# Weight sums of a Strassen-like product: DMA accumulation and ScalarE negatives in place of GpSimd and VectorE subtractions

## The chip, the cores and the metric

The kernel runs on one core of a Trainium2 chip. Such a core has a matrix engine (TensorE, PE in the profile, with its weight loads as PEld), three elementwise engines (VectorE or DVE, ScalarE or ACT, GpSimd or POOL), a queue that only issues transfers (SyncE, SP) and 16 DMA engines. Each engine takes its instructions in order. The metric is the device time of one execution in microseconds (us); lower is better.

## The reference, cut to what matters

The first half is a state-space scan over `x` of 4 batches x 8 heads x 768 tokens x 32, in chunks of 32 tokens; its output is laid out as 3,072 tokens x 256 features. The second half is a feed-forward block, and only its last product matters for the change:

```python
h = x @ w_in                                   # 3072 x 256  times  256 x 2048
g = np.where(h > 0.0, h, np.exp(np.minimum(h, 0.0)) - 1.0)
return (g @ w_out).astype(np.float32)          # 3072 x 2048 times 2048 x 256
```

`w_out` is float32, 2048 x 256.

## The kernel before, in words

The tokens are worked through in twelve blocks of 256, numbered n = 0 to 11; from n = 2 on two blocks go as a pair. For each pair the kernel computes the scan (decays, scores, state sums and products, on all engines), then the first product `l1` / `l1_words` (L663, L781), the activation in several steps on ScalarE and VectorE, and the second product with `w_out`. The weights come in by DMA as pieces, are rounded and recombined on ScalarE, VectorE and GpSimd, and stay in SBUF.

The second product has two forms. Blocks 0 and 1 use `l2` (L828), an ordinary accumulation over 16 slices of `w_out`, each slice 128 x 256. All later pairs use `second` (L874), which splits `w_out` into quarters a11, a12, a21 and a22 (each of 8 rows of 128 x 128, 128 features by 128 columns; L724 and L725: an even or odd slice, and its left or right half of columns) and multiplies seven combinations in place of eight quarters, in the manner of Strassen's method as Winograd wrote it. It needs four sums of weights, computed once:

- s1 = a21 + a22, written over a21
- s2 = s1 - a11
- s3 = a11 - a21 (with the old a21)
- s4 = a12 - s2

s2, s3 and s4 lie in three new tiles of 128 x 8 x 128 (`weight_sums`, L720), s1 in the place of a21. `l2` still reads the old a21, so row i of s1 can only be written after block 1's `l2(1, i)`.

The order of the work is written out by hand. The code around the change is:

- the loop over j = 0 to 7 (L1179): blocks 2 and 3 through `l1`, block 0 through `l2(0, j)`, the last weight pieces, and the scan of the pair 4, 5 ahead (`scan_ahead`, L1147: with `decay`, whose exponentials are L525 on ScalarE and whose masks are L530 on GpSimd). After j = 7 come `words_of_w(5)` and `low_of_w(5)` (L735, L745), which split a piece of `w_in` into words; the latter is two subtractions on GpSimd (L851).
- the loop over j = 8 to 15, i = j - 8 (L1231): the pair 2, 3 through `l1_words`, block 1 through `l2(1, i)`, at i = 0 the scaling of B for blocks 4 and 5 (`scaled`, L406, GpSimd's L412, into the tile b_tok), at i = 2 their scores, state sums (`sums`, matmuls of L575 from b_tok) and states (L592 on VectorE, L597 on GpSimd), and at i = 4 and 5 their outputs (`across` L608 and `inside` L628, with the copies L655 to yT on ScalarE). At i = 7 `words_of_y(4)` and `both_of_y(4)` (L766, L776 on VectorE) turn yT into words for the next pair.
- the loop for n = 4 and on (L1312): the pair n through `l1_words` while `second(n - 2)` runs in steps (`l2s`). Its seven products per half are numbered r = 0 to 6 and use a11, a12, s1, s2, s3, a22 and s4 in that order; the first half takes rows 0 to 3 of each, the second rows 4 to 7. The additions to its results are L888 on VectorE.

In the kernel before, `differences` (L1175) puts s3's rows on GpSimd at i = 0, 2, 3 and 5; `sum_weights` (L709) puts the other three sums of row i on GpSimd at i = 0 to 5; and the rows 6 and 7 are left to VectorE in the loop for n = 4, two steps at each of k = 2, 3 and 4 (`left`, L1289, and L1325). All of them are TENSOR_TENSOR instructions of 128 x 128. Each `l1_words` is followed by L799, L808 and L809 on ScalarE and L802 and L816 on VectorE, for the activation.

Of the kernel before, what the change touches and what calls it, by code (L numbers as in the profile page):

```python
# [14 lines left out]
ALU = mybir.AluOpType  # L15
ACT = mybir.ActivationFunctionType
# [16 lines left out]
def kernel(  # L33
# [27 lines left out]
    nc = tc.nc  # L61
# [30 lines left out]
    for k in range(4):  # L92
        (nc.scalar if k % 2 else nc.sync).dma_start(
            out=la0[BH * k:BH * (k + 1)],
            in_=a.rearrange("b h (c s) -> (b h) c s", s=P)[:, 0:2, :])
# [187 lines left out]
    for v in range(2):  # L283
        nc.gpsimd.affine_select(
            out=low16[Q * v:Q * v + Q], in_=low16[Q * v:Q * v + Q], pattern=[[1, Q]],
# [5 lines left out]
        out=hmask, in_=hmask, pattern=[[-N, NH]], compare_op=ALU.is_ge, fill=0.0,  # L291
        base=0, channel_multiplier=1)
    nc.gpsimd.affine_select(
        out=hmask, in_=hmask, pattern=[[N, NH]], compare_op=ALU.is_ge, fill=0.0,
# [8 lines left out]
        out=minus, in0=ident, scalar1=-1.0, scalar2=None, op0=ALU.mult)  # L303
# [213 lines left out]
    def decay(n, q):  # L517

        decay_of(n, 2 * q)
        decay_of(n, 2 * q + 1)  # L520
# [165 lines left out]
    def elu():  # L686
        if not begun:
            begin_elu()
        n, i, ps = lag.pop(0)
        e = begun.pop()  # L690
        nc.scalar.activation(e, e, ACT.Exp, scale=-1.0)
        g_of[n, i] = ffn.tile([P, 2, BLK], F32, tag=f"g{n % 2}", name="g", bufs=12)
        nc.vector.scalar_tensor_tensor(
            out=g_of[n, i], in0=e, scalar=1.0, in1=ps,
            op0=ALU.subtract, op1=ALU.max)
# [10 lines left out]

    def sum_weights(eng, a, s, i):  # L709
        for step in weight_steps(eng, a, s, i):  # L710
            step()

    def weight_steps(eng, a, s, i):
        a11, a12, a21, a22 = (part[:, i] for part in a)
        s2, _, s4 = (part[:, i] for part in s)
        for out, in0, in1, op in (
                (a21, a21, a22, ALU.add), (s2, a21, a11, ALU.subtract), (s4, a12, s2, ALU.subtract)):
            yield lambda: eng.tensor_tensor(out=out, in0=in0, in1=in1, op=op)

    def weight_sums():  # L720
        return [conv.tile([P, MC // 2, P], F32, tag="w64", name="w_sum", bufs=W_AHEAD)
                for _ in range(3)]

    w_parts = w_out.rearrange("p (i k) (r c) -> p k r i c", k=2, c=P)  # L724
    a_out = [w_parts[:, k, r] for r in range(2) for k in range(2)]  # L725
    s_out = []
# [8 lines left out]
    def words_of_w(i):  # L735

        w = pieces[i][0]
        k_words[i] = conv.tile(
            [P, 2, KC, CW], F32R, tag="w64", name="w_words", bufs=W_AHEAD)
        nc.scalar.activation(k_words[i][:, 0], w, ACT.Copy, scale=NEAR)  # L740
        nc.vector.scalar_tensor_tensor(
            out=k_words[i][:, 1], in0=k_words[i][:, 0].bitcast(F32), scalar=1.0 / WORD - 1.0,
            in1=w, op0=ALU.mult, op1=ALU.add)

    def low_of_w(i):  # L745

        w0 = conv.tile([P, KC, CW], F32R, tag="w_in", name="w0", bufs=DF // CW + 1)
        for k in range(KC):
            sub(w0[:, k], pieces[i][0][:, k], k_words[i][:, 0, k].bitcast(F32))
        k_words[i] = k_words[i], w0  # L750
# [99 lines left out]
    def sub(out, in0, in1):  # L850
        nc.gpsimd.tensor_tensor(out=out, in0=in0, in1=in1, op=ALU.subtract)  # L851
# [120 lines left out]
    def w_take(i, low):  # L972

        w_abs(i)
        w_low(i, low)
        w_sign(i)

    def w_give(i):

        w_high(i)  # L980
        w_sum(i)
# [190 lines left out]
            at = k // 2 * 2 + late  # L1172
            turn_part(*[(m, 0), (m, 1), (m, 2), (m + 1, 0), (m + 1, 1), (m + 1, 2), (m, 3), (m + 1, 3)][at])

    def differences(i, count):  # L1175
        for r in range(i, i + count):
            sub(s_out[1][:, r], a_out[0][:, r], a_out[2][:, r])

    for j in range(2 * DIRECT):  # L1179
        n, i = 2 + j // DIRECT, j % DIRECT  # L1180
        if j < 7:
            l2(0, j)
        piece = todo < len(pieces) and j != 1
        if j == 0:
            elu()
        if piece:
            w_take(todo, nc.vector)
        l1(n, i)
        if j == 7:
            l2(0, j)  # L1190
        if j == 0:
            scaled(3, nc.gpsimd)
            turn(3)
            elu()
            turn_exp(3)
        if piece:
            w_give(todo)
            todo += 1
        while lag:
            elu()  # L1200
        if j == 4:
            w_take(todo, nc.scalar)
            w_give(todo)
            todo += 1
        if j == 0:
            decay(3, 2)
            decay(3, 3)
        if j == 1:
            scores(3)
            sums(3)  # L1210
            for q in range(4):
                weigh(3, q)
        if j == 2:
            states(3)
        if j == 3:
            inside(across(3), 3)
        if j == 4:
            words_of_y(2)
        if j == 4:
            words_of_w(4)  # L1220
        if j == 5:
            low_of_w(4)
        if j == 5:
            both_of_y(2)
        scan_ahead(j)
        if j == 3:
            s_out[:] = weight_sums()
        if j == 7:
            words_of_w(5)
            low_of_w(5)  # L1230
    for j in range(8, 16):  # L1231
        i = j - 8
        l1_words(2, j, between=4 if i == 7 else None)
        for p in ((), (6,), (), (7,), (0,), (1,), (2,), ())[i]:
            words_of_w(p)
        for p in ((), (), (6,), (7,), (0,), (), (), ())[i]:
            low_of_w(p)
        if i == 7:
            l2(1, 6)
            l2(1, 7)  # L1240
        begin_end()
        if i == 0:
            turn_part(5, 2)
            scaled(4, nc.gpsimd)
            scaled(5, nc.gpsimd)
        if i < 2:
            load_bc(i + 6)
            l2(1, i)
        if i == 2:
            l2(1, 2, half=0)  # L1250
            scores(4, 5)
            sums(4, 5)
            for q in range(4):
                weigh_two(4, q)
            l2(1, 2, half=1)
            states(4)
            states(5)
            turn_part(4, 3)
            turn_part(5, 3)
            for to in (6, 7):  # L1260
                load_b(to)
                spread_cum(to)
        if i == 3:
            l2(1, 3)
        if i == 4:
            y = across(4, 5)
            inside(y, 4, 5, ts=(0,))
            l2(1, 4)
        if i == 5:
            l2(1, 5, half=0)  # L1270
            inside(y, 4, 5, ts=(1,))
            l2(1, 5, half=1)
        if i in (0, 1, 3, 4):
            sum_t1(2, (0, 1, 3, 4).index(i), nc.vector)
        if i in (4, 6):
            turn_part(6, i // 2 - 2)
        if i in (0, 2, 3, 5):
            differences((0, 0, 2, 4, 0, 6)[i], 2)
        if i < 6:
            sum_weights(nc.gpsimd, a_out, s_out, i)  # L1280
    end_words()
    for p in (1, 2):
        low_of_w(p)
# [2 lines left out]
    low_of_w(3)  # L1286
    sum_t2(2, 0)
    sub(g_of[2, 14][:, 1], g_of[2, 14][:, 1], g_of[2, 14][:, 0])
    left = (step for i in (6, 7) for step in weight_steps(nc.vector, a_out, s_out, i))  # L1289

    def stage_scan(n, k):

# [19 lines left out]
    for n in range(4, NP, 2):  # L1312
        m = n + 2 if n + 2 < NP else None
        steps = second(n - 2)

        def l2s(count):
            for _ in range(count):
                next(steps)

        for k in range(16):  # L1320
            l1_words(n, k, between=m if k == 15 else None)
            turn_step(n, k // 2 * 2 + 1, k % 2)
            if n == 4 and k == 0:
                decay(6, 1)
            if n == 4 and 1 < k < 5:  # L1325
                for _ in range(2):
                    next(left)()
            if m:
                stage_scan(n, k)
            begin_end()  # L1330
            if k == 0 and n > 4:
                store(n - 4, 0)
                store(n - 4, 1)
            if not m:
                l2s(4 if k % 2 else 3)
                continue
            l2s((3 + (n == 4), 3 - (n == 4), 3, 3, 3, 3, 3, 3, 4, 5, 2, 2, 3, 1, 1, 0)[k])
            if k == 9:
                scores(m, m + 1)
                sums(m, m + 1)  # L1340
                for q in range(4):
                    weigh_two(m, q)
                l2s(2)
                states(m)
            if k == 10:
                states(m + 1)
            if k == 13:
                y = across(m, m + 1)
                inside(y, m, m + 1, ts=(0,))
                l2s(4)  # L1350
                inside(y, m, m + 1, ts=(1,))
        if m:
            l2s(4)
            both_of_y(m)
        end_words()
        for _ in steps:
            pass
    n = NP - 2
# [34 lines left out]
```

## Time and profile before

| | |
|---|---|
| median of 3 runs | 350.58 us (350.37 to 350.59) |
| profiled execution | 350.72 us, of it 348.8 us span |
| granted TensorE clock | 0.999 |
| GpSimd: 8 subtractions for s3 (L851, w_sum<-w_out) | 4.3 us, 552 ns each |
| GpSimd: 18 sums at L718 | 3.6 + 3.4 + 3.1 us, 605, 567 and 524 ns each |
| VectorE: 6 sums at L718 | 125.7 to 133.1 us |
| first product with s2 (ps_o<-w_sum,t) | 126.4 us |
| first product with s3 (ps_o<-w_sum,g) | 130.6 us |
| busy from 87 to 100 us: PE, DVE, ACT, POOL | 12.56, 12.07, 6.29, 12.60 us of 13 |
| busy from 100 to 115 us | 14.67, 12.88, 11.73, 14.37 us of 15 |
| busy from 115 to 125 us | 9.83, 7.00, 8.25, 9.78 us of 10 |
| busy from 125 to 135 us | 9.30, 9.93, 8.46, 9.77 us of 10 |

The span runs from the first to the last instruction of the profiled execution. Busy times say how full an engine is in a stretch; for TensorE the ends of instructions are modelled, so full means that no idle time was seen. Times in timelines count from the start of the span. A line such as L851 can be that of a helper, so groups are told apart by their tiles: `w_sum<-w_out` are the weight sums, `w<-w_in,w_words` the low words of `w_in`, `g<-g`, `t<-g`, `g<-t,g` and `g<-g,t` the sums of activations for `second`.

### The profile page before, as it was taken

The numbers are of one execution on the slowest core, as the hardware profiler recorded it, in microseconds if no ns is written. First come the engines' busy times: TensorE is split into PE (matmuls) and PEld (weight loads), VectorE is DVE, ScalarE is ACT, GpSimd is POOL, SyncE is SP. The second block draws the span as 40 slices with busy tenths as digits, with TensorE's granted clock in tenths as the row PEclk, the third lists the DMA queues.
The fourth block names the chain that finished last, engine by engine and source line by source line (L and its number), as shares of the span: only waits on it lengthen the run. The fifth ranks groups of instructions, "written<-read, shape, count | busy, mean of one in ns | idle before, by whom it ended". The sixth has DMA issues, their size and how long they took to land.

```text
span 348.8 us, 9876 instructions
## 1 busy us (share of the span) xinstructions
PE 340.7 (98%) x3878; PEld 298.3 (86%) x3878; DVE 258.5 (74%) x514; ACT 235.2 (67%) x538; POOL 219.4 (63%) x338
## 2 busy tenths in 40 slices
PE   8999999999999999999999999999999999999996
PEld 5669888888878788888999988998988999999996
DVE  3998989879987799875878775888675756665232
ACT  4789989599748789647699447699557566665000
POOL 5554554558999998964196864196854174455860
PEclk9999999999999999999999999999999999999999
DMA  8988988551360601080431070320000100001002
GB/s 148 238 217 181 309 187 226 123 93 43 65 137 2 131 22 31 7 156 12 103 64 32 8 158 6 95 44 2 2 0 5 62 0 3 0 0 43 22 0 62
DMA packets 72727, 26.49 MB, mean 76 GB/s; under 512 B 57768, under 2 KB 67560, under 8 KB 72680
## 3 DMA queue, kind: packets, MB, share of 16 engines
q1 hardware_dynamic: 70360, 25.60, 31.6%
q8 instruction: 30, 0.49, 0.6%
q10 hardware_dynamic: 2320, 0.26, 0.5%
q14 instruction: 17, 0.14, 0.1%
HBM read 22.51 MB, written 3.34 MB: 74 GB/s over the span
## 4 chain that ended last, share of the span: by engine, by line
PE 80%; DVE 7%; ACT 6%; SPq 2%; DMA 2%; issue 2%; POOL 0%; DVEq 0%; ACTq 0%; POOLq 0%
PE ps_o L910 32%; PE ps_h L791 16%; PE ps_h L671 11%; PE ps_w L791 8%; PE ps_o L835 6%; PE ps_y L638 2%; DVE ps_h L802 2%; DMA w<-in_moe_w_in_dram 2%; ACT e L809 1%; ACT e L808 1%; PE ps_g L545 1%; PE ps_y L620 1%; PE ps_st L575 1%; ACT e L799 1%; ACT L L525 1%
## 5 line engine op out<-in xcount | busy, mean ns | idle before, releaser
L910 PEld LDWEIGHTS ps_o<-w_out,g 128*128 128x128 f32 x640 | 78.6, 191 | 3.6 <-ACT p_sum L922 0.2
L910 PE MATMUL ps_o<-w_out,g 128*128 128x128 f32 x640 | 80.3, 275 | 0.0
L808 ACT ACTIVATE e<-ps_h 128x512 f32<-128x512 f32 x72 | 43.0, 597 | 53.5 <-DVE ps_h L802 53.5
L816 DVE SCALAR_TENSOR_TENSOR g<-e,ps_h 128x512 f32<-128x512 f32 x72 | 49.3, 685 | 30.6 <-ACT e L809 30.1
L851 POOL TENSOR_TENSOR g<-g 128x256 f32<-128x256 f32 x36 | 27.2, 757 | 57.2 <-DVE g L816 56.9
L802 DVE SCALAR_TENSOR_TENSOR ps_h<-ps_h,e 128x512 f32<-128x512 f32 x72 | 50.0, 695 | 13.9 <-ACT e L799 11.3
L799 ACT ACTIVATE e<-ps_w 128x512 f32<-128x512 f32 x72 | 42.2, 586 | 14.4 <-PE ps_w L791 14.3
L791 PE MATMUL ps_w<-y_both,w_words 128*128 128x512 f32 x144 | 51.2, 435 | 0.5 <-DVE y_both L776 0.4
L809 ACT ACTIVATE e<-e 128x512 f32<-128x512 f32 x72 | 45.5, 632 | 2.3
L671 PE MATMUL ps_h<-yT,w_in 128*128 128x256 f32 (+1 forms) x208 | 45.2, 368 | 1.3 <-POOL w_in L252 1.3
L791 PE MATMUL ps_h<-y,w_words 128*128 128x512 f32 x144 | 46.1, 401 | 0.1
L791 PE MATMUL ps_h<-y,w 128*128 128x512 f32 x144 | 44.6, 391 | 0.0
L671 PEld LDWEIGHTS ps_h<-yT,w_in 128*128 128x128 f32 x208 | 36.3, 190 | 7.4 <-POOL w_in L252 2.6
L525 ACT ACTIVATE L<-L,ncum 128x64 f32<-128x64 f32 x160 | 42.2, 336 | 0.2
L910 PE MATMUL ps_o<-w_sum,g 128*128 128x128 f32 x304 | 38.5, 275 | 0.9 <-DVE p_sum L888 0.7
L910 PEld LDWEIGHTS ps_o<-w_sum,g 128*128 128x128 f32 x304 | 37.0, 192 | 2.5 <-POOL g L851 0.9
L530 POOL TENSOR_SCALAR_AFFINE_SELECT L<-L 64x512 f32<-64x512 f32 x40 | 29.6, 741 | 11.0 <-ACT L L525 9.7
L791 PEld LDWEIGHTS ps_h<-y,w 128*128 128x128 f32 x144 | 27.0, 188 | 6.4
L851 POOL TENSOR_TENSOR g<-t,g 128x256 f32<-128x256 f32 x40 | 28.1, 736 | 5.8 <-PE ps_o L910 5.7
L791 PEld LDWEIGHTS ps_h<-y,w_words 128*128 128x128 f32 x144 | 26.5, 188 | 5.9 <-PE ps_w L791 0.5
L835 PE MATMUL ps_o<-w_out,g 128*128 128x256 f32 x128 | 30.9, 383 | 0.0
L851 POOL TENSOR_TENSOR t<-g 128x256 f32<-128x256 f32 x40 | 29.1, 759 | 0.3
(134 smaller groups left out, 540.4 us busy)
## 6 DMA issues: line engine op xcount, KB each, us to landing
L<-flat SPq DMA_DIRECT2D x20, 256.0 KB
w<-in_moe_w_out_dram SPq DMA_DIRECT2D x8, 512.0 KB
w<-in_moe_w_in_dram SPq DMA_DIRECT2D x7, 512.0 KB
xr<-in_x_dram SPq DMA_DIRECT2D x24, 128.0 KB
out_dram<-c_sum SPq DMA_DIRECT2D x9, 256.0 KB
bc<-in_B_dram SPq DMA_DIRECT2D x24, 64.0 KB
bc<-in_C_dram SPq DMA_DIRECT2D x22, 64.0 KB
ec<-flat_exp SPq DMA_DIRECT2D x10, 128.0 KB
```

Of the source, the lines that this page charges most:

```text
L525: nc.scalar.activation(L[:, h, u], L[:, h, u], ACT.Exp, bias=ncum[:, u, row:row + 1])
L530: nc.gpsimd.affine_select(out=part, in_=part, pattern=[[0, 4], [0, 2], [1, Q]], compare_op=ALU.is_ge, fill=0.0, base=0, channel_multiplier=-1)
L671: nc.tensor.matmul(out=ps[:, j, toks], lhsT=w_in[i][:, k, j * P:(j + 1) * P], rhs=yT[n // 2][:, k, n % 2].rearrange("p u i -> p (u i)")[:, ...
L791: nc.tensor.matmul(out=ps, lhsT=lhs[:, k], rhs=rhs[:, k], start=k == 0 and lhs is not w0, stop=k == KC - 1 and lhs is not w1)
L799: nc.scalar.activation(e, both, ACT.Copy, scale=WORD)
L802: nc.vector.scalar_tensor_tensor(out=high, in0=high, scalar=WORD - 1.0, in1=e, op0=ALU.mult, op1=ALU.add)
L808: nc.scalar.activation(e, high, ACT.Relu, scale=-1.0)
L809: nc.scalar.activation(e, e, ACT.Exp, scale=-1.0)
L816: nc.vector.scalar_tensor_tensor(out=g_of[n, m].rearrange("p b i -> p (b i)"), in0=e, scalar=1.0, in1=h, op0=ALU.subtract, op1=ALU.max)
L835: nc.tensor.matmul(out=o_of[n][:, ts], lhsT=g_of[n, j][:, m % 2, ts * P:(ts + 1) * P], rhs=w_out[:, m], start=(m == 0 and ts == 0), stop=( ...
L851: nc.gpsimd.tensor_tensor(out=out, in0=in0, in1=in1, op=ALU.subtract)
L910: nc.tensor.matmul(out=ps[:, ts], lhsT=b[:, ts * P:(ts + 1) * P], rhs=a[:, i], start=(i == chunk[0] and ts == 0), stop=(i == chunk[-1]), s ...
```

## The change

Two helpers replace the subtractions. `less(out, in_)` writes the negative of a tile on ScalarE; `plus(out, in_, rows)` issues, from GpSimd's queue, a transfer from SBUF to SBUF that adds its source to its destination. With them the sums become

- s3 = -a21 (ScalarE, j = 6), then s3 += a11 (transfer, j = 7)
- s2 = -s3 (ScalarE, i = 2), then s2 += a22 (transfer, i = 3)
- s4 = -s2 (ScalarE, i = 5), then s4 += a12 (transfer, i = 6)
- a21 += a22, rows 0 to 3 at i = 5 and rows 4 to 7 after the loop, ahead of n = 4 (two transfers)

Each of the negatives and of the first three transfers covers all eight rows at once, 128 x 1024 float32 or 512 KB, in runs of 512 bytes. A negative of s3 or of s2 needs the transfer before it to have landed. `differences`, `sum_weights`, `weight_steps` and VectorE's `left` go away.

```diff
-    def sum_weights(eng, a, s, i):
-        for step in weight_steps(eng, a, s, i):
-            step()
-
-    def weight_steps(eng, a, s, i):
-        a11, a12, a21, a22 = (part[:, i] for part in a)
-        s2, _, s4 = (part[:, i] for part in s)
-        for out, in0, in1, op in (
-                (a21, a21, a22, ALU.add), (s2, a21, a11, ALU.subtract), (s4, a12, s2, ALU.subtract)):
-            yield lambda: eng.tensor_tensor(out=out, in0=in0, in1=in1, op=op)
+    def less(out, in_):
+
+        nc.scalar.activation(out, in_, ACT.Copy, scale=-1.0)
+
+    def plus(out, in_, rows=slice(None)):
+
+        nc.gpsimd.dma_start(out=out[:, rows], in_=in_[:, rows], accum_op=ALU.add)
...
-    def differences(i, count):
-        for r in range(i, i + count):
-            sub(s_out[1][:, r], a_out[0][:, r], a_out[2][:, r])
-
     for j in range(2 * DIRECT):
...
         if j == 3:
             s_out[:] = weight_sums()
+        if j == 6:
+            less(s_out[1], a_out[2])
         if j == 7:
             words_of_w(5)
+            plus(s_out[1], a_out[0])
             low_of_w(5)
     for j in range(8, 16):
...
-        if i in (0, 2, 3, 5):
-            differences((0, 0, 2, 4, 0, 6)[i], 2)
-        if i < 6:
-            sum_weights(nc.gpsimd, a_out, s_out, i)
+        if i == 2:
+            less(s_out[0], s_out[1])
+        if i == 3:
+            plus(s_out[0], a_out[3])
+        if i == 5:
+            less(s_out[2], s_out[0])
+            plus(a_out[2], a_out[3], slice(0, 4))
+        if i == 6:
+            plus(s_out[2], a_out[1])
...
-    left = (step for i in (6, 7) for step in weight_steps(nc.vector, a_out, s_out, i))
+    plus(a_out[2], a_out[3], slice(4, 8))
...
-            if n == 4 and 1 < k < 5:
-                for _ in range(2):
-                    next(left)()
```

## The prediction

> **What bounds the kernel now.** I read the engines' busy times first, then the chain of work that ended last, then the timelines of POOL, PE and ACT around the edited lines, and the waits.
>
> The page's line of busy times:
>
> ```profile
> PE 340.7 (98%) x3878; PEld 298.3 (86%) x3878; DVE 258.5 (74%) x514; ACT 235.2 (67%) x538; POOL 219.4 (63%) x338
> ```
>
> TensorE is the bound, and its stream has few holes. The busy times by stretch put its idle time from 87 to 150 us at 0.44 + 0.33 + 0.17 + 0.70 + 0.74 = 2.4 us. All edits act in this stretch or just ahead of it, so 2.4 us is about the most that they can win.
>
> The chain of work in that stretch (start us, us, what):
>
> ```profile
> 92.47 0.66 PE ps_st L575 x45
> ...
> 97.30 0.48 PE ps_w L791 x2
> 97.78 0.97 DVE bct L448 x2
> ...
> 108.22 0.37 ACT yT L655
> 108.59 0.03 issue
> 108.61 0.60 ACT e L799
> ...
> 113.39 1.74 DVE y_both L776 x2
> 115.13 0.04 issue
> 115.17 0.50 PE ps_w L791
> ```
>
> To 97.8 us the chain is TensorE's. From 97.78 to 115.17 it alternates between DVE and ACT: there a delay on ACT reaches TensorE through y_both.
>
> The timelines (start, us, engine, line, out<-in; in brackets the idle time before and its releaser), first ACT, then POOL, then PE:
>
> ```profile
> 82.90 0.59 ACT L841 COPY ob<-ps_o 128x512 f32<-128x512 f32 x1
> 99.99 0.60 ACT L808 ACTIVATE e<-ps_h 128x512 f32<-128x512 f32 x1 [4.18 <-DVE ps_h L802]
> ```
> ```profile
> 85.68 1.72 POOL L530 TENSOR_SCALAR_AFFINE_SELECT L<-L 64x512 f32<-64x512 f32 x2 [0.90 <-ACT L L525]
> 87.48 2.06 POOL L851 TENSOR_TENSOR w<-w_in,w_words 128x256 fp32r<-128x256 f32 x2
> 89.51 1.72 POOL L412 TENSOR_TENSOR b_tok<-b_tok,eb 128x256 f32<-128x256 f32 x2
> ```
> ```profile
> 99.40 0.81 PE L620 MATMUL ps_y<-bct,Sx 32*64 32x64 f32 x52 [0.44 <-DVE g L816]
> 115.17 0.50 PE L791 MATMUL ps_w<-y_both,w_words 128*128 128x512 f32 x1 [0.36 <-DVE y_both L776]
> 130.66 1.13 PE L910 MATMUL ps_o<-w_sum,g 128*128 128x128 f32 x8 [0.70 <-DVE p_sum L888]
> ```
>
> POOL works without a break from 85.7 us to past 130. b_tok, which TensorE multiplies at 92.47, is ready at 91.23: a reserve of 1.24 us. The holes that can close are those of 0.44, 0.36 and 0.70 us.
>
> **Part by part.** Removed from POOL: 8 differences (4.3 us) and 18 steps at L718 (3.6 + 3.1 + 3.4), 14.4 us, all after 91.19. Removed from DVE: the six steps of rows 6 and 7 at L718, 0.76 + 0.71 + 0.30 + 0.81 + 0.67 + 0.72 = 4.0 us between 125.7 and 133.1. Two of them end just ahead of the p_sum addition that TensorE awaits at 130.66: that hole of 0.70 us goes, and I also take the 0.17 us that PE waits for ACT's c_sum at 138.78, behind the same DVE queue. Together -0.87 us.
>
> Added to ACT: three negatives of 128x1024. Rows of 128x512 follow one another after 0.54 us and those of 128x64 (L525) after 0.24, so 512 more columns cost 0.34: estimate 0.9 us each. The first (j = 6) comes between L525 and the copy of ob at 82.90. That copy would end at 84.3; l2 starts at 84.09, so TensorE loses 0.2 us. ACT was full there (4.00 us of 4.00 from 80 to 84), hence all of ACT, and DVE and POOL's L530 behind it, move by 0.8. The second (i = 2) falls into ACT's idle 4.18 us before 99.99 and costs nothing while its operand has landed. The third (i = 5) stands between the yT copies and L799 at 108.61, on the chain: 0.9 us.
>
> Added to POOL: five transfers, three of 1,024 runs of 512 bytes and two of 512 runs. No POOL-issued transfer exists in this trace, so its time T on POOL for 1,024 runs must be bounded. Below nothing is excluded, since each issue is an instruction of its own in POOL's queue. Low end: SP issues a load of x, also 1,024 runs, in 0.58 us (median). High end: POOL's two-input rows take 741 ns for 256 columns, 2.9 ns a column; a run at one column's price, once for each of the two reads, is 2 x 1,024 x 2.9 ns = 6 us. I take 3 us, one column's price for each run, because the row that is nearest in kind is POOL's own software pace, and 1.5 us for the half ones. The Trainium skill, in "DMA: Bandwidth & Descriptors", section "Anatomy of one DMA — SWDGE (gpsimd) path", holds that generating descriptors on this path is a small part of the cost and that many can be emitted before it shows. No run here shows that; it would put T near its low end and the time at 350.6 or below (the first rival).
>
> Where T counts: the transfer of j = 7 stands after L530 and ahead of w L851 and b_tok L412. b_tok is then ready at 91.23 + 0.8 + T = 92.03 + T, and TensorE, in order, waits with everything behind it: a shift of T - 0.44, for T = 3 of 2.56 us. DVE loses 0.8 through ACT, and gains the 0.82 us that it idles at 97.57 for POOL's Sx, since the differences ahead of Sx are gone. So from 97.78 the DVE chain is where it was, TensorE comes later, and its holes of 0.44 and 0.36 us close: 2.56 - 0.80 = 1.76 at 115.2. The DVE/ACT chain with the third negative moves by 0.9, and by 1.5 with TensorE's later y products ahead of L655: less than 1.76, so it is covered by TensorE's own delay. If T were under 2.1 us, that cover would be gone and the 0.9 would be the shift instead.
>
> The later transfers meet a relieved POOL: with T = 3, 3 + 3 + 1.5 + 3 + 1.5 = 12 us against 14.4. Queued behind them on POOL are w L851, g L851, Sx and L530; the subtractions for r = 4 end at 128.45, 2.2 us before use, which holds.
>
> Landing: loads moved 226 GB/s at a DMA share of 0.89 from 8 to 15 us, so about 254 GB/s; 512 KB read twice takes 4.1 us. ACT can wait for the first transfer until about 97.8 (0.9 for the negative and 0.6 for L799 before DVE's L802 at 99.27), 6.6 us after its issue ends; for the second until 109.2, 7.1 us after 102.1. Both hide. SP's queue is not touched. A further DMA queue may change what lies around the span (350.72 - 348.8 = 1.9 us); I take nothing, within the range.
>
> **Sum.** The profiled execution took 350.72 us: + 2.56 - 0.80 - 0.87 = + 0.89, 351.6 us. Its own time is 0.14 above the median of the runs, 350.58, so I say 351.5 us, 0.26% slower. What a measurement can tell from no change is about 0.2%, 0.7 us.
>
> **Rivals.**
> - Cheap issue, faster: T near 0.6 us. TensorE loses only 0.2 at 84, and the third negative's 0.9 on the chain is met by DVE rows that no longer run beside POOL: L741 took 0.94 us at 109.85 and 0.68 at 90.06, and L766 and L776 (3.4 us for four) fall on the 4.0 us of L851 and L718 rows removed from 111.35 to 115.4; at the 0.6 us spacing of undisturbed rows they would save about 0.9. Then only -0.87 stays: 349.7. It decides where T is under 1 us. Against it: POOL has other subtractions waiting to move into that place.
> - POOL becomes the bound: T of 5 us or more. At 6, TensorE is 5.56 - 0.80 = 4.76 late at 115; POOL emits 24 us for 14.4 saved and is 0.8 late, 10.4, of which 2.2 + 4.76 is reserve: 3.4 us more at r = 4, and 0.70 does not return. About 358.8; at 5 us 353.6. For it: two reads for each run.
> - Late landing: an accumulating transfer needs more than 7 us. At 10, ACT stands before the third negative from 109.2 to 112.1, L799 comes 4.4 late and TensorE with it: 4.4 - 0.87 = + 3.5, 354.1. For it: broadcasts hold the DMA engines at 0.91 from 96 to 100. Against it: from 104 to 112 they are idle.
>
> **Chances.** Forecast (T from 1.5 to 4.5, 350.4 to 353): 0.42, of it 0.02 faster, 0.15 within 0.2%, 0.25 slower. Cheap issue: 0.25, of it 0.19 faster and 0.06 same. POOL as the bound: 0.20, late landing: 0.13, both slower. Faster 0.21, same 0.21, slower 0.58. The range reaches from the cheap case, 349.7, to 357, which leaves out the worst of the second rival (0.07) and what lies below (0.1). The forecast's own range is 350.4 to 353.
>
> **What would show it.** Right: POOL idle for about 3 us after L530 at 88; PE's first ps_st matmul waiting about 2.3 us for POOL's b_tok; no hole before r = 4 at 130; ACT idle before neither later negative. The forecast is wrong if that ps_st wait is absent (T under 1), if PE waits for POOL's g at r = 4 (T over 5), or if ACT stands before the negatives (landing).

## The result, and the profile after

Six executions of the changed kernel took 354.37 us in the median (353.40 to 355.06), against 350.48 us (350.05 to 351.42) for six of the kernel before on the same chip: a ratio of 1.0108, 95% interval 1.0087 to 1.0129. The change makes the kernel slower by 3.9 us. The profiled execution took 354.04 us, 0.3 below the median, with a span of 351.9 us; its granted clock was 0.993.

Line numbers of the helpers after the change are 3 lower than before from L741 on (L851 is now L848, L802 is L799, L776 is L773, L864 is L861). L711 is the negative and L715 the transfer.

The busy times on the page of the kernel after:

```profile
PE 342.1 (97%) x3878; PEld 299.1 (85%) x3878; DVE 257.4 (73%) x508; ACT 237.7 (68%) x541; POOL 212.9 (61%) x317
```

POOL was relieved by 6.5 us and DVE by 1.1, ACT took 2.5 more, and yet the span is 3.1 us longer.

The view of one tile, w_sum, of the kernel after (line, engine, operation, duration of one in ns as min/median/max, first and last start) shows the new instructions:

```profile
L715 POOL DMA_DIRECT2D w_sum<-w_out x3: 1550/1552/1768, 88.4 to 111.6; - x3
L711 ACT ACTIVATE w_sum<-w_sum x2: 1058/1058/1059, 97.6 to 110.2; 128x1024 f32<-128x1024 f32 x2
...
DMA to landing us min/median/max: 6.5/7.1/9.1
```

A transfer of 1,024 runs holds POOL for 1.55 to 1.77 us, a negative takes 1.06 us on ACT, and a transfer lands 6.5 to 9.1 us after its issue.

The chain of work that ended last, in the kernel after, around the place where before it ran from 97.78 to 115.17 through DVE and ACT (start us, us, what):

```profile
101.28 0.94 PE ps_y L638 x53
102.23 0.03 issue
102.26 0.68 DVE g L813
...
104.41 1.00 DVE g L861
...
109.84 0.36 ACT yT L655
110.20 0.02 issue
110.23 1.06 ACT w_sum L711
111.29 0.49 ACT e L796
111.78 0.02 issue
111.80 0.55 DVE ps_h L799
```

The chain leaves TensorE at 102.23 and comes back to it only with the words of y at 118.11: 15.9 us on DVE and ACT, with the third negative in the middle of it.

The timelines of POOL and then of PE in the kernel after (start, us, engine, line, operation, out<-in; in brackets the idle time before and its releaser):

```profile
86.74 1.72 POOL L530 TENSOR_SCALAR_AFFINE_SELECT L<-L 64x512 f32<-64x512 f32 x2 [1.58 <-ACT L L525]
88.42 1.77 POOL L715 DMA_DIRECT2D w_sum<-w_out  x1
90.26 1.42 POOL L848 TENSOR_TENSOR w<-w_in,w_words 128x256 fp32r<-128x256 f32 x2
91.65 1.86 POOL L412 TENSOR_TENSOR b_tok<-b_tok,eb 128x256 f32<-128x256 f32 x2
...
111.59 1.55 POOL L715 DMA_DIRECT2D w_sum<-w_out  x1 [2.21 <-ACT w_sum L711]
112.50 5.00 POOL L848 TENSOR_TENSOR w<-w_in,w_words 128x256 fp32r<-128x256 f32 x4
```
```profile
91.05 0.50 PE L788 MATMUL ps_h<-y,w 128*128 128x512 f32 x1 [0.39 <-POOL w L848]
91.73 0.50 PE L788 MATMUL ps_h<-y,w 128*128 128x512 f32 x1 [0.18 <-POOL w L848]
...
115.93 0.48 PE L788 MATMUL ps_h<-y,w 128*128 128x512 f32 x1 [0.42 <-DVE y L763]
117.07 0.46 PE L788 MATMUL ps_h<-y,w 128*128 128x512 f32 x1 [0.66 <-DVE y L763]
118.11 1.39 PE L788 MATMUL ps_w<-y_both,w_words 128*128 128x512 f32 x2 [0.58 <-DVE y_both L773]
119.31 3.13 PE L907 MATMUL ps_o<-w_out,g 128*128 128x128 f32 x16
```

TensorE waits for POOL at 91, as the forecast had it, though for the low words of `w_in` and not for b_tok. It then waits for DVE's words of y from 115 to 118. The first sixteen products of `second` start at 119.31, where they started at 115.51 before, and take 3.13 us where they took 1.95. The row of the kernel before:

```profile
115.51 1.95 PE L910 MATMUL ps_o<-w_out,g 128*128 128x128 f32 x16
```

DVE on the way there in the kernel after, then the partners of these rows in the kernel before:

```profile
98.65 0.85 DVE L448 TENSOR_TENSOR bct<-bct,ec 128x256 f32<-128x256 f32 x2
...
104.34 1.84 DVE L861 TENSOR_TENSOR g<-g 128x256 f32<-128x256 f32 x1
...
111.80 0.70 DVE L799 SCALAR_TENSOR_TENSOR ps_h<-ps_h,e 128x512 f32<-128x512 f32 x1 [1.91 <-ACT e L796]
112.41 1.37 DVE L738 SCALAR_TENSOR_TENSOR w_words<-w_words,w_in 128x512 fp32r<-128x512 f32 x1
...
114.76 2.16 DVE L763 SCALAR_TENSOR_TENSOR y<-y,yT 128x512 fp32r<-128x512 f32 x2
116.84 1.81 DVE L773 SCALAR_TENSOR_TENSOR y_both<-y,yT 128x512 fp32r<-128x512 f32 x2
```
```profile
103.16 0.96 DVE L864 TENSOR_TENSOR g<-g 128x256 f32<-128x256 f32 x1
...
109.25 0.70 DVE L802 SCALAR_TENSOR_TENSOR ps_h<-ps_h,e 128x512 f32<-128x512 f32 x1 [0.97 <-ACT e L799]
109.85 0.94 DVE L741 SCALAR_TENSOR_TENSOR w_words<-w_words,w_in 128x512 fp32r<-128x512 f32 x1
...
111.78 1.61 DVE L766 SCALAR_TENSOR_TENSOR y<-y,yT 128x512 fp32r<-128x512 f32 x2
113.31 1.80 DVE L776 SCALAR_TENSOR_TENSOR y_both<-y,yT 128x512 fp32r<-128x512 f32 x2
```

The lateness of the words of y can be added up from these rows. L861 starts 1.18 late (103.16 before); 0.37 of it was there at 81 us already, before any edit acts, and such a start differs from execution to execution. It takes 1.84 instead of 0.96, which adds 0.88; 0.42 of that is taken up at L802 (105.56 before), where DVE had stood waiting for ACT. So the copies of yT on ACT start 1.62 late (109.08 against 107.46). The negative adds 0.96 (L796 follows L711 by that), and L799 starts 2.55 late. L738, L763 and L773 take 5.34 us together instead of 0.94 + 1.61 + 1.80 = 4.35: another 0.99. The end of y_both is then 118.65 against 115.11, 3.54 late.

From 122 us on the kernel makes some of it good: TensorE is 4.97 late at 122.19 (against 117.22) and about 3.1 at the end of the span.

The busy times by stretch of the kernel after (stretch; busy us and count of PE, PEld, DVE, ACT, POOL; granted clock, DMA share, GB/s):

```profile
116.00:120.00 4.00, 2.74 (x8) 1.65 (x9) 3.87 (x5) 0.10 (x1) 1.51 (x2) 0.80 1.00 198
120.00:124.00 4.00, 4.00 (x24) 3.74 (x24) 2.14 (x4) 3.97 (x13) 2.19 (x3) 0.78 0.83 139
...
125.00:135.00 10.00, 10.00 (x67) 9.03 (x66) 6.98 (x13) 9.20 (x25) 9.85 (x14) 1.00 0.29 42
135.00:150.00 15.00, 15.00 (x219) 13.58 (x218) 12.34 (x26) 12.41 (x30) 14.55 (x22) 1.00 0.05 16
```

Behind TensorE's holes the granted clock falls to 0.80 and 0.78 for two stretches of 4 us. It did not fall before. From 125 to 150 us TensorE has no hole left; before it lacked 0.70 and 0.74 us there.

### The profile page after: what moved, and what is told of

It reads as the page before. It is cut to its first block, busy times and chain, and to the rows that moved or that the text cites. A ratio compares the mean times of both kernels' runs of the same rounds, so it can differ in the third digit from the quotient of the medians.

```text
span 351.9 us, 9859 instructions
## 1 busy us (share of the span) xinstructions
PE 342.1 (97%) x3878; PEld 299.1 (85%) x3878; DVE 257.4 (73%) x508; ACT 237.7 (68%) x541; POOL 212.9 (61%) x317
## 4 chain that ended last, share of the span: by engine, by line
PE 81%; ACT 7%; DVE 4%; SPq 2%; DMA 2%; issue 1%; POOL 1%; DVEq 0%; ACTq 0%; POOLq 0%
PE ps_o L907 36%; PE ps_h L788 17%; PE ps_w L788 9%; PE ps_h L671 9%; PE ps_o L832 3%; PE ps_y L638 2%; ACT L L525 2%; DMA w<-in_moe_w_in_dram 2%; PE ps_g L545 2%; PE ps_y L620 1%; PE ps_st L575 1%; ACT e L684 1%; DVE w_words L738 1%; ACT yT L655 1%; SPq L179 1%
## 5 line engine op out<-in xcount | busy, mean ns | idle before, releaser
L907 PEld LDWEIGHTS ps_o<-w_out,g 128*128 128x128 f32 x640 | 79.9, 194 | 3.5
L907 PE MATMUL ps_o<-w_out,g 128*128 128x128 f32 x640 | 81.3, 278 | 0.0
L848 POOL TENSOR_TENSOR g<-g 128x256 f32<-128x256 f32 x36 | 26.3, 732 | 59.1 <-DVE g L813 58.7
L799 DVE SCALAR_TENSOR_TENSOR ps_h<-ps_h,e 128x512 f32<-128x512 f32 x72 | 50.0, 694 | 14.2 <-ACT e L796 11.4
L796 ACT ACTIVATE e<-ps_w 128x512 f32<-128x512 f32 x72 | 42.2, 586 | 13.8 <-PE ps_w L788 13.7
L788 PE MATMUL ps_h<-y,w 128*128 128x512 f32 x144 | 45.4, 394 | 1.7 <-DVE y L763 1.1
L530 POOL TENSOR_SCALAR_AFFINE_SELECT L<-L 64x512 f32<-64x512 f32 x40 | 30.7, 768 | 10.6 <-ACT L L525 9.3
L848 POOL TENSOR_TENSOR g<-t,g 128x256 f32<-128x256 f32 x40 | 28.0, 733 | 5.8 <-PE ps_o L907 5.7
L848 POOL TENSOR_TENSOR t<-g 128x256 f32<-128x256 f32 x40 | 29.1, 759 | 0.3
```

The lines of the kernel that those rows point to most:

```text
L530: nc.gpsimd.affine_select(out=part, in_=part, pattern=[[0, 4], [0, 2], [1, Q]], compare_op=ALU.is_ge, fill=0.0, base=0, channel_multiplier=-1)
L788: nc.tensor.matmul(out=ps, lhsT=lhs[:, k], rhs=rhs[:, k], start=k == 0 and lhs is not w0, stop=k == KC - 1 and lhs is not w1)
L796: nc.scalar.activation(e, both, ACT.Copy, scale=WORD)
L799: nc.vector.scalar_tensor_tensor(out=high, in0=high, scalar=WORD - 1.0, in1=e, op0=ALU.mult, op1=ALU.add)
L907: nc.tensor.matmul(out=ps[:, ts], lhsT=b[:, ts * P:(ts + 1) * P], rhs=a[:, i], start=(i == chunk[0] and ts == 0), stop=(i == chunk[-1]), s ...
```

## The experiments

Two readings of this were set against each other; the expectations call them P and Q. P: the loss is the first transfer, which holds the low words and so all of TensorE at 91 us; what comes later only follows. Q: the loss is the third negative and the transfer that waits for it. They lengthen the chain to the words of y, push the low words beside DVE's steps, and open the hole after which the clock falls.

| kernel | edit against the changed kernel | median, us | before, us | ratio, 95% interval |
|---|---|---|---|---|
| changed kernel | none | 354.37 | 350.48 | 1.0108 [1.0087, 1.0129] |
| e1_neg_later | third negative and its transfer later | 351.10 | 350.59 | 1.0019 [1.0010, 1.0028] |
| e6_tr_later | only the transfer of these later | 352.50 | 350.50 | 1.0050 [1.0037, 1.0064] |
| e2_fill | TensorE's hole filled | 353.82 | 350.59 | 1.0089 [1.0072, 1.0107] |
| e5_no_first | first transfer left out | 353.00 | 350.59 | 1.0087 [1.0059, 1.0116] |
| e7_first_early | first transfer earlier | 353.83 | 350.50 | 1.0090 [1.0075, 1.0104] |
| e9_first_early_fill | e7 and e2 together | 353.77 | 350.25 | 1.0090 [1.0073, 1.0107] |
| e10_second_early | e9, second transfer earlier | 352.70 | 350.52 | 1.0067 [1.0053, 1.0081] |
| e8_both | e1 and e7 together | 351.21 | 350.50 | 1.0015 [1.0004, 1.0027] |
| e3_no_transfers | all five transfers left out | 350.27 | 350.59 | 0.9988 [0.9979, 0.9998] |
| e4_no_sums | negatives left out too | 349.10 | 350.50 | 0.9958 [0.9945, 0.9971] |
| c0_left_pool | kernel before, VectorE's six sums on GpSimd | 349.68 | 350.25 | 0.9979 [0.9971, 0.9988] |
| c1_s1_only | s1 alone by transfers | 349.46 | 350.25 | 0.9978 [0.9964, 0.9992] |

**The third negative and its transfer later.** The negative moves behind the last copy of ob in the loop (i = 7), the transfer behind the loop.

```diff
-            less(s_out[2], s_out[0])
             plus(a_out[2], a_out[3], slice(0, 4))
-        if i == 6:
-            plus(s_out[2], a_out[1])
...
             l2(1, 7)
+            less(s_out[2], s_out[0])
...
+    plus(s_out[2], a_out[1])
     plus(a_out[2], a_out[3], slice(4, 8))
```

> The third negative (s4 = -s2) moves from i = 5, between the yT copies and the next l1_words evacuation, to i = 7 after the copy of ob, where ScalarE idles 4.6 us in the changed kernel; its transfer moves behind the loop. Everything else stays. Theory Q (the chain from ScalarE and VectorE to the y words sets the time, the hole it leaves on TensorE from 114 to 119 us lowers the granted clock to 0.8, and that costs again): the y words come 1 us earlier for the negative and some more because GpSimd's transfer issue at 111.6 us no longer delays its subtractions into VectorE's y words; hole at least halved, clock near 1.00: 351.3 to 352.8 us. Theory P (as predicted: the first transfer in GpSimd's queue ahead of the low words and of b_tok delays TensorE by 1.2 us at 91 us, and that carries the loss): nothing of it is touched, 353.8 to 354.6 us.

It took 351.10 us, 3.3 less than the changed kernel and slightly under Q's range. P's value is excluded. VectorE, POOL and PE of this kernel, in that order:

```profile
111.51 0.68 DVE L738 SCALAR_TENSOR_TENSOR w_words<-w_words,w_in 128x512 fp32r<-128x512 f32 x1
...
113.18 1.63 DVE L763 SCALAR_TENSOR_TENSOR y<-y,yT 128x512 fp32r<-128x512 f32 x2
114.74 1.28 DVE L773 SCALAR_TENSOR_TENSOR y_both<-y,yT 128x512 fp32r<-128x512 f32 x2
```
```profile
108.96 1.93 POOL L848 TENSOR_TENSOR w<-w_in,w_words 128x256 fp32r<-128x256 f32 x2
111.52 2.14 POOL L848 TENSOR_TENSOR w<-w_in,w_words 128x256 fp32r<-128x256 f32 x2 [0.64 <-POOL w L848]
```
```profile
91.09 0.49 PE L788 MATMUL ps_h<-y,w 128*128 128x512 f32 x1 [0.39 <-POOL w L848]
...
116.41 1.95 PE L907 MATMUL ps_o<-w_out,g 128*128 128x128 f32 x16
```

The wait at 91 is as long as in the changed kernel, so it is not what costs the 3.3 us. The subtractions L848 run from 108.96, 3.5 us earlier, since no transfer stands ahead of them waiting for a negative. The three DVE groups take 3.59 us instead of 5.34, and `second` starts at 116.41. Its sixteen products take 1.95 us again: the clock stayed at 1.00.

**Only the transfer later.** The negative stays at i = 5, and `plus(s_out[2], a_out[1])` alone moves behind the loop.

> Half of the last step: the third negative stays at i = 5, between the yT copies and L796; only its transfer moves behind the loop. If the negative's own 0.96 us on the chain is the loss at 115 us: 353.4 to 354.4 us, as the changed kernel. If it is the transfer in GpSimd's queue, which waits for that negative (2.21 us) and holds the low words of two pieces back until they meet VectorE's y words (L738, L763 and L773 took 1.37 + 2.16 + 1.81 us there, and 0.68 + 1.63 + 1.28 with the pair of edits moved): those rows shrink by about 1.7 us and the time is 351.4 to 352.6 us.

It took 352.50 us, between the two kernels around it. So the place of the transfer in POOL's queue is worth 354.37 - 352.50 = 1.9 us, what the lowered clock cost included, and the place of the negative on ACT another 352.50 - 351.10 = 1.4. The split holds for this order of the two edits; no run moves the negative alone. The three DVE groups are at 0.68, 1.64 and 1.28 us here too: their slowing belongs to the held transfer and the subtractions behind it, not to the negative.

The Trainium skill, "SBUF — State Buffer", section "SBUF: two separate sides", has a VectorE instruction with two SBUF inputs and a GpSimd instruction that reads SBUF exclude each other for a whole instruction. The traces of the changed kernel agree in part: L861 took 0.41 us at 89.06, while POOL issued a transfer, and 0.95 at 101.38 beside L848. But its 1.84 at 104.34 and L738's 1.37 at 112.41 both stand where L848 starts 0.9 us behind a transfer; in the kernel with only the transfer later, L738 and L848 start together (112.55 and 112.56) and L738 takes 0.68. So the transfer issued just ahead has a share in these two rows, and no run prices it apart.

**The hole filled.** Four products without use, with the identity, are put into the first `l1_words` for n = 4, between its passes, to keep TensorE busy while it waits for the words of y (`first` is n == 4 and m == 0, `at` counts the passes).

```diff
             for k in range(KC):
+                fill = (0, 0, 4, 2, 2, 3)[2 * at + k] if first else 0
+                if fill:
+                    nc.tensor.matmul(
+                        out=ps_fill[:, 0:fill], lhsT=ident,
+                        rhs=ident.unsqueeze(1).to_broadcast([P, fill, P]), start=True, stop=True)
```

> The changed kernel with four matrix products without use (identity times identity, 4.1 us in the trace's rate at most) put into the hole that TensorE has between the y passes of block pair 4's first slice, at about 115.5 to 119 us. Nothing else moves. If the granted clock of 0.80 and 0.78 from 116 to 124 us follows from the hole: the clock stays near 1.00 there and the products after it run at their usual pace, 1.0 to 1.3 us less: 352.9 to 353.5 us. If the clock is lowered for another reason: 354.2 to 355.0 us, the products without use adding up to 0.5.

The clock stays at 1.00, the sixteen products start at 119.38 as before the edit (119.31) and take 2.04 us instead of 3.13. With the hole filled the lowered clock thus stays away. Of the 1.1 us the medians show 0.55 won: 353.82 lies between the two ranges, the intervals of the two ratios overlap, and the two profiled executions took the same time (354.01 and 354.04). The rest turns up as new waits: ACT stands 0.48 us before the third negative, and TensorE waits later. Two stretches of this kernel:

```profile
116.00:120.00 4.00, 3.86 (x17) 2.32 (x16) 3.92 (x5) 0.04 (x1) 1.56 (x2) 1.00 1.02 198
...
145.00:150.00 5.00, 4.42 (x149) 3.91 (x147) 3.93 (x11) 3.31 (x7) 4.85 (x8) 1.00 0.01 3
```

In the second stretch TensorE is idle for 0.58 us; in the changed kernel it had no hole there. By the medians the lowered clock costs about half a microsecond of the 3.9, less than Q had for it.

**The first transfer left out** (s3 is then only -a21).

> Only the first transfer (s3 += a11 at j = 7) is left out, so s3, s2 and s4 lack a11 and the output is not the reference's. Theory P: TensorE no longer waits for GpSimd's low words at 91 us and the loss shrinks by the 1.2 us of that wait or more: 352.5 to 353.2 us. Theory Q: TensorE comes earlier to a hole that the chain of ScalarE and VectorE sets, the hole grows by as much and the time stays: 353.9 to 354.8 us.

It took 353.00 us: three executions within 0.05 of that and one at 354.76. The median lies in P's range. By the medians the first transfer costs about 1.4 us, near the shift of 1.23 that TensorE has at 92 us. But the intervals of the two ratios overlap, and what the 1.4 consists of is not that shift alone: in the profiled execution the words of y are ready 0.86 us earlier than in the changed kernel (117.79 against 118.65, of which 0.51 was there at 81 us), and the clock stayed at 1.00, so that the sixteen products took 1.95 us. So P seems to have a part, though the smaller one; its size is not shown.

**The first transfer earlier.** POOL idles for 1.58 us before L530 at 86.74. The transfer goes there.

```diff
+        if j == 7:
+            plus(s_out[1], a_out[0])
         scan_ahead(j)
...
             words_of_w(5)
-            plus(s_out[1], a_out[0])
             low_of_w(5)
```

> Only the place of the first transfer changes: it is issued ahead of the decays of j = 7, where GpSimd waits 1.58 us for ScalarE's L525, instead of ahead of the low words. GpSimd's 1.77 us then lies in a gap and TensorE's waits for the low words at 91 us (0.39 and 0.18 us and the loads before them, 1.2 us in all) go. Theory P: 352.5 to 353.3 us. Theory Q, with the chain setting the time at 115 us: 353.2 to 354.4 us; what it wins there is what VectorE and ScalarE get from coming earlier. The run without the first transfer stood at 353.0.

It took 353.83 us, in Q's range: by the medians 0.5 won where leaving the transfer out won 1.4, and the intervals overlap here too. The transfer starts at 84.75 and TensorE's waits at 91 are gone. The reason stands in ACT's timeline of this kernel:

```profile
108.40 1.12 ACT L655 COPY yT<-ps_y 128x256 f32<-128x256 f32 x3
110.12 1.06 ACT L711 ACTIVATE w_sum<-w_sum 128x1024 f32<-128x1024 f32 x1 [0.59 <-DMA w_sum<-w_out]
```

ACT arrives at the third negative 0.7 us earlier than in the changed kernel (0.3 of it was there at 81 us) and then waits 0.59 us for the second transfer to land. The negative starts at 110.12 instead of 110.23.

**Both first early and filled.** The fill was added to this kernel, to see whether the clock (0.50 and 0.65 in the stretches from 116 to 124) had eaten the gain.

> The first transfer in GpSimd's gap (353.83 us, clock 0.50 and 0.65 from 116 to 124 us) with the same four products without use in TensorE's hole as in the earlier run. If the lowered clock took back what the earlier issue won at 91 us: the clock stays near 1.00 and the time falls to 352.3 to 353.2 us. If the later holes would have been there anyway, as after the first filling (0.5 us won, not 1.2): 353.3 to 353.8 us.

It took 353.77 us, in the second range. The clock is 1.00 throughout and the time is the same. But ACT waits 1.02 us for the landing here, and the words of y come 0.48 later than without the fill, about what the fill had won before (0.55); so this run does not tell what the lowered clock alone had cost.

**The second transfer earlier.** One line moves, so that the second transfer is issued in POOL's idle 0.96 us at 98.5.

```diff
             less(s_out[0], s_out[1])
-        if i == 3:
             plus(s_out[0], a_out[3])
```

> Against the kernel with the first transfer early and the four filling products (353.77 us), the second transfer is issued one step earlier, at i = 2, right behind the negative that it adds to, where GpSimd idles 0.96 us at 98.5. In that kernel ScalarE stood 1.02 us in front of the third negative, at 110.60, for the landing of the second transfer. Theory L, a late landing ate what the early first transfer won: the wait is gone, the third negative follows the copies of yT at 109.6 or before, the y words come about 1.0 us earlier (VectorE's L738 at 111.8 instead of 112.78), and the time is 352.4 to 353.2. Rival, something behind the y words sets the end anyway: the wait is gone too, but the time stays at 353.5 to 354.1. A third outcome, 352.3 or less, would say that the collision of the low words with VectorE's step on g (1.81 us at 103.75) moved as well.

It took 352.70 us, in the range of a late landing. ACT's timeline of this kernel:

```profile
108.09 1.13 ACT L655 COPY yT<-ps_y 128x256 f32<-128x256 f32 x3
109.24 1.06 ACT L711 ACTIVATE w_sum<-w_sum 128x1024 f32<-128x1024 f32 x1
```

The wait is gone, and the negative starts 1.36 us earlier than in the kernel that it is compared with. Of this 1.02 is the wait and 0.34 comes from the step on g, which takes 0.96 us at 103.74 instead of 1.81 at 103.75. It still runs beside a subtraction of the low words, but no transfer is issued just ahead of that one any more. The intervals of the two ratios overlap, so the gain of 1.1 us rests on the medians; that the wait was there and went is in the traces.

**Third negative late and first transfer early.**

> Both moves together, the third negative and its transfer behind the places where they hurt and the first transfer in GpSimd's gap; the output is the reference's. From 351.1 (negative and transfer moved) about 1.2 us of the wait at 91 us can return, less what the chain at 115 us takes back: 350.0 to 350.6 us. If below 350.2 it beats the kernel before; if TensorE's wait at 91 us was covered by later holes, it stays at 350.9 to 351.2.

It took 351.21 us in the median, no less than with the first of the two edits alone. Its twelve executions spread from 350.30 to 352.44, and the profiled one was among the fastest (350.45). What the spread comes from stays open.

**No transfers, and no sums.** First the five `plus` are left out and the negatives kept, then the negatives as well; the products then take the unsummed weights.

> The three negatives stay, the five transfers are left out, so the sums lack their second terms and the output is not the reference's. Theory Q: GpSimd issues nothing and its subtractions come earlier, ScalarE still has its 0.96 us on the chain: TensorE loses about 1 us at 115 us and wins back the holes after 130: 350.3 to 351.5 us. Theory P: the loss was the wait for GpSimd, so all of it goes and the relief shows: 349.5 to 350.3 us. If the transfers cost next to nothing: 353.5 to 354.5 us.

> No sums at all: the products take quarters of w_out in place of s1 to s4, so the output is not the reference's; no negatives, no transfers, no subtractions. It shows the most that any way of making the sums can win against the kernel before: by its holes at 99, 115, 130, 138 and 146 us (0.44 + 0.36 + 0.70 + 0.17 + 0.57 us recorded) between 348.4 and 349.8 us.

They took 350.27 and 349.10 us. The five transfers cost 4.1 us, more than the whole loss; the three negatives without them cost 1.2; and the sums for nothing would be worth 1.4 us against the kernel before. That last bounds what a change to the sums alone can win, with the rest in its place. The first value lies just inside P's range and 0.03 us under Q's, and tells nothing between them.

**The other direction.** Two kernels start from the one before. In the first only VectorE's six sums go to GpSimd, at k = 6 to 8; no transfer and no negative is in it.

```diff
-    left = (step for i in (6, 7) for step in weight_steps(nc.vector, a_out, s_out, i))
+    left = (step for i in (6, 7) for step in weight_steps(nc.gpsimd, a_out, s_out, i))
...
-            if n == 4 and 1 < k < 5:
+            if n == 4 and 5 < k < 9:
```

> The kernel before, with one edit: the six sums of rows 6 and 7 leave VectorE at k = 2 to 4 of the loop for n = 4 and go to GpSimd at k = 6 to 8, two at each. No transfer, no negative. It measures by itself what taking those six instructions off VectorE is worth, which the forecast put at -0.87 us (TensorE's holes of 0.70 us at 130 and 0.17 at 138): 349.5 to 350.0 us if so, 350.3 to 350.7 if those holes are made up elsewhere.

It took 349.68 us against 350.25, a ratio of 0.9979: 0.6 to 0.7 us faster than the kernel before, in the range that was set for it and near the 0.87 of the prediction. A stretch of it:

```profile
125.00:135.00 10.00, 10.00 (x67) 9.01 (x66) 7.18 (x15) 9.06 (x24) 9.77 (x15) 1.00 0.09 27
```

TensorE's 0.70 us of idle time in this stretch is gone. In the second kernel s1 is made by its two transfers, s2 as a22 - s3 and the rest on GpSimd.

> The kernel before, with s1 = a21 + a22 alone by two transfers (rows 0 to 3 after i = 5, rows 4 to 7 behind the loop), the others as subtractions on GpSimd with s2 = a22 - s3, rows 6 and 7 at k = 6 and 7. No negative on ScalarE, no transfer ahead of the low words, eight sums fewer on GpSimd and VectorE for 2.6 us of issue. If a transfer pays where it needs no negative and stands ahead of nothing: 349.2 to 350.0 us, under the run with the rows only moved. If GpSimd's relief is worth nothing where TensorE is the bound: as that run within 0.2 us.

It took 349.46 us, with the same ratio, 0.9978. Two transfers of half the size at harmless places cost nothing that can be measured, and win nothing either. Both kernels beat the one before.

## Why the prediction was right and wrong

The sign was right, and 354.37 lies in the range of 349.7 to 357.0. The likeliest case was not: it said +0.9 and reached to 353, and the measured difference is +3.9. The range reached so far for two rivals, POOL as the bound and a late landing, and neither is what the runs show as the main cause; the late landing even gave 354.1. So that the time lies in the range is luck as far as the mechanism goes.

- **T and the first transfer.** T was taken as 3 us; it is 1.55 to 1.77, and 1.26 to 1.29 for 512 runs. The formula gave the right size: T - 0.44 is 1.1 to 1.3, and TensorE's row at 92.07 lies 1.23 behind what it was before the edit took hold (1.76 late there, of it 0.53 already at 84). But the waiter was misnamed, so the agreement is partly luck. It is the product with the low words (0.39 + 0.18 us for POOL's L848), ahead of b_tok's, so the announced wait at ps_st was absent although T was not under 1. That sign was badly chosen: it stood for one waiter of two.
- **The cover of the third negative: the step that failed.** "The DVE/ACT chain with the third negative moves by 0.9, and by 1.5 with TensorE's later y products ahead of L655: less than 1.76, so it is covered by TensorE's own delay". It moved by 3.5 (3.2 without the 0.37 that was there at 81), and TensorE's own delay, the cover, was 1.0 and not 1.76 (110.67 against 109.64). The 0.9 was right (0.96), and by the forecast's own rule a T under 2.1 made it the shift. Two things were missing. The chain was not where it was when the negative came: "from 97.78 the DVE chain is where it was" failed, for DVE's rows L592 were 1.61 late (96.94 against 95.33) and not 0.8, L448 was still 0.88 late after the gain at Sx (98.65 against 97.77), and L861 beside the low words behind the second transfer made it 1.62 at the copies of yT. To that the 0.96 is added. And the third transfer's place in POOL's queue was counted only by its issue: it waits 2.21 us for the negative, holds four low-word subtractions until 112.50, and these then run beside L738, L763 and L773. The runs put 1.9 us on that place and, after it, 1.4 on the negative's.
- **The recovery of 0.8.** The hole of 0.44 at 99.4 did close. The one of 0.36 at 115.2 did not: holes of 0.42 to 0.66 took its place.
- **VectorE's steps removed, -0.87.** About right: -0.6 to -0.7 where it was done alone, and no hole after 125 us in the changed kernel.
- **The first negative.** 0.2 us on TensorE was forecast and 0.16 is seen (0.37 late at 81, 0.53 at 84).
- **Landing.** The estimate was 4.1 us, the measured times 6.5, 7.1 and 9.1. The first landed so late that ACT stood 2.05 us before the second negative (97.56). The forecast had named this as a sign against it, but it is covered: ACT was idle there before. The second landed just in time, about 0.2 us before ACT was ready for it (102.88 + 7.1 = 109.98 against 110.21). Issued at this place it landed after 7.1 to 8.3 us from kernel to kernel, and where the work ahead was earlier or the landing later it set the chain (e2, e7, e9). So the rival "late landing" did not decide the changed kernel, but was right that 7 us is where it begins. From 95 to 112 us the accumulating transfers and SP's loads share the DMA engines; two lines of the transfers' view of the kernel after for that stretch (packets, MB, share of the 16 engines):

```profile
q0 software_dynamic: 1664, 0.83, 44.0%
q1 hardware_dynamic: 4574, 1.36, 40.8%
```

44% of 17 us for 0.83 MB is 111 GB/s of engine time, so 512 KB needs 4.7 us of all 16 engines even alone. The size was nearly right; the loads beside it were left out. That they are the cause is argued from these lines; no run took the loads away. The Trainium skill, "DMA: Bandwidth & Descriptors", section "Anatomy of one DMA — SWDGE (gpsimd) path", gives 2.0 us and bytes over 436 GB/s for one transfer, here an estimate of 3.2 us; the measurement is two to three times that.
- **The rivals.** "Cheap issue" put T at 0.6 us and set its limit at 1, and the rows take 1.55 to 1.77, though after two of the transfers POOL's next instruction started within 0.95. It named the DVE rows that collide with POOL, but expected them to be freed, which is what happened with the third transfer out of the way (3.59 us) and the reverse of what happened with it in the queue. "POOL becomes the bound" failed: T was far from 5 us, and TensorE had no hole from 125 to 150 us, where r = 4 lies. (Its 353.6 for 5 us does not come out of its own terms, 350.58 + 3.76 + 0.44 = 354.8; nothing hangs on it.)
- **The clock.** No step of the forecast had it. By the medians of the filling run it cost about 0.5 us.

## What to carry to other kernels

A transfer that GpSimd issues takes a place in its order: here one waited 2.21 us for its operand, everything behind it waited too, and what was freed late then ran beside, and slowed, the very chain that was already late. Before calling an added instruction covered, add up all delays that lie on its chain, and ask for each queue what the held instructions will collide with. Here the sums were cheap where they stood, 1.4 us for all of them; moving six of them from a full VectorE to a later place on GpSimd won 0.6 to 0.7 us, while replacing them all lost 3.9.

## What the runs showed of the hardware

- A transfer with 1,024 runs occupies POOL for 1.55 to 1.77 us in its row, but the next instruction started 0.91 to 0.95 us after a transfer at 102.88 and 111.59, and 1.84 after the one at 88.42. VectorE's two-input step beside the issue at 89 was not slowed (0.41 us); L738, begun 0.8 us after the transfer at 111.59 and with L848 behind it, took 1.37.
- Accumulating transfers from SBUF to SBUF landed after 6.5 to 9.7 us for 512 KB, and after 4.2 us in the median for 256 KB (7.9 to 8.0 where one was issued right behind another, in e1, e6 and e8).
- TensorE's granted clock fell to 0.80 and 0.78, and in e7_first_early to 0.50 and 0.65, behind holes of 0.3 to 1.4 us that followed one another from 114 to 118 us, and was back at 1.00 in the stretch from 124. In e5_no_first the holes in the stretch from 112 to 116 were larger (PE busy 2.11 us of 4, against 3.06) and the clock stayed at 1.00 in the profiled execution. What decides it stays open. The Trainium skill, "TensorE: Matmul & The Clock Gate", section "What's actually happening", names two clocks, full and half, and an activity window of about 3.4 us that runs freely; 0.50 over a whole stretch agrees with a half clock, and a window that falls differently on the holes would agree with the difference between the two kernels, but no run here shows it.
